# A first load split in two halves over two issuing engines, in a recurrence followed by a soft mixture of experts

## Chip, cores and metric

The kernel runs on one core of one Trainium2 chip. The metric is the device time of one execution in microseconds (us). A core has a matrix engine (PE, TensorE), a vector engine (DVE, VectorE), a scalar engine (ACT, ScalarE), a general engine (POOL, GpSimd) and a synchronising engine (SP, SyncE) that does no arithmetic. Transfers between the chip's memory and the on-chip buffer of 128 partitions are issued by SP, ACT or POOL, each with a queue of its own, and carried out by 16 DMA engines.

## The reference

Two layers in a row. The first is a gated recurrence over 5056 tokens for each of 4 sequences and 256 channels, the second a soft mixture of 8 experts with 4 slots each over all 20224 tokens.

```
x: (4, 5056, 256)   f_logit: (4, 5056, 256)   lower_bound: (256)
phi: (256, 32)      w1: (8, 256, 1024)        w2: (8, 1024, 256)      all float32

sig = 1 / (1 + exp(-f_logit))
f   = lower_bound + (1 - lower_bound) * sig
i   = 1 - f
h   = 0
for t in range(5056):
    h = f[:, t] * h + i[:, t] * x[:, t]
    y[:, t] = h

x = y.reshape(20224, 256)
logits = x @ phi
d = softmax of logits over the tokens
slot_input = d.T @ x
for each expert e:  slot_out[e] = relu(slot_input[e] @ w1[e]) @ w2[e]
c = softmax of logits over the 32 slots
out = c @ slot_out
```

## The kernel before

**Tiling.** The tokens of each sequence are cut into groups of 512 (128 partitions times 4 tokens). One group of one sequence is a unit; units are numbered with the sequence running fastest, 40 in all. A pair of units shares a tile of `f_logit` (`f_t`) and a tile of `x` (`x_t`), each 128 partitions by 2 by 4 by 256 values in float32; three tiles of each kind are in rotation. The first six units (`SINGLE`, L318) are loaded one at a time: one transfer of 512 KB for each half of a tile, 128 rows of 4 KB. In the middle a transfer brings a whole pair, 1 MB, and a group near the end has a shape of its own.

**What a unit passes through.** `gate` (L227): ACT takes the sigmoid of `-f_logit` into `s_t`. `enter` (L237): `u_t = s_t * x_t`, on DVE in two parts for unit 0, on POOL for the others. `s_to_channels` and `u_to_channels`: PE transposes both so that channels lie on partitions. `decay` (L286): ACT turns the transposed sigmoid into the decay `a` with a scale taken from `lower_bound` and a bias of 1. `scan` (L306): DVE runs the recurrence. `to_tokens`, `keep_tokens`, `logits`, `exps`, `weights_to_tokens` and `slots` then build the softmax over the tokens and gather the slot inputs on PE, ACT and DVE.

**Constants.** `lower_bound` comes as a row of 256 values, `lb_row`, by a transfer that ACT issues at L75, at the start of the program. `lb_constants` (L104) transposes that row with two small PE instructions (L109) and makes `omlb` and `nomlb`, the two signs of `1 - lower_bound`, with two DVE instructions (L110, L111). `decay` scales with `nomlb`; `phi_constants` (L113) multiplies `phi`, which POOL loads at L79, by `omlb`.

**Loads.** `load(n, k)` (L204) runs over `f_logit` and `x` in that order and issues every load from SP. For the first units it is the last branch, L224 and L225. A load into a tile in rotation is issued when the tile's last reader is done with it. Weights are loaded by POOL (`load_w`, L135), cast to bf16 on the way, at units listed in `W_AT`; the last two second-layer weights use a tile of `f_t`'s rotation and are named `w_t`.

**Order.** The order on each engine is written out by hand; each engine runs its instructions in program order and waits for semaphores. At the beginning (L462 on) all six single loads are issued on SP, twelve transfers in the order f, x, f, x; then follow `lb_constants`, `gate(0)`, `enter(0)`, `s_to_channels(0)`, the first half of `decay(0)`, `u_to_channels(0)`, `gate(1)`, and so on. On ACT's queue the issue of `lb_row` is therefore followed by the loading of the function table for the sigmoid and then by the sigmoid of unit 0. On PE the two transposes of `lb_row` come ahead of those of `s_t`; on DVE the two constants come ahead of unit 0's multiply.

**The end.** When the last weights are there, PE finishes `so_ps` (L669), DVE and POOL make `slot_out` and `slot_bd` (L683, L685), and the output is formed block by block: a matmul, a scaling on DVE or ACT, and a store issued by SP (L724, L744, L763, L789, L806).

Of the kernel before, what the change touches and what calls it, by code (L numbers as in the profile page):

```python
# [18 lines left out]
def kernel(  # L19
# [10 lines left out]
    nc = tc.nc  # L30
# [5 lines left out]
    P = 128  # L36
# [9 lines left out]
    def first(g):  # L46
        return g * G if g < n_grp - 1 else S - G
# [24 lines left out]
    rep = consts.tile([P, B, NS], F32, name="rep")  # L72

    lb_row = consts.tile([1, D], F32, name="lb_row")
    nc.scalar.dma_start(out=lb_row, in_=lower_bound.unsqueeze(0))  # L75
    lbs = consts.tile([P, 2, DC], F32, name="lbs")
    omlb, nomlb = lbs[:, 0], lbs[:, 1]
    phi_f = consts.tile([P, DC, NS], F32, name="phi_f")
# [25 lines left out]
    def lb_constants():  # L104
        row = lb_row.rearrange("u (p o) -> u p o", o=DC)
        lb_ps = ptp.tile([P, R, P], F32, name="lb_ps", tag="tp")
        lb = lb_ps[:, 0, ds(0, DC)]
        for o in range(DC):
            nc.tensor.transpose(lb_ps[:, 0, ds(o, 1)], row[:, :, o], ident_f[ds(0, 1), ds(0, 1)])  # L109
        nc.vector.tensor_scalar(omlb, lb, -1.0, 1.0, ALU.mult, ALU.add)  # L110
        nc.vector.tensor_scalar(nomlb, lb, 1.0, -1.0, ALU.mult, ALU.add)  # L111
# [50 lines left out]
    with tc.tile_pool(name="sp2", bufs=3) as sp2, \  # L162
# [24 lines left out]
        def long(n):  # L187
            return 2 * B <= n < n_unit - 2 * B

        def place(n):  # L190
            if long(n):
                t, j = divmod(n, 2 * B)
                return 2 * t + j % 2, j // 2
            return divmod(n, B)
# [4 lines left out]
        def tokens(src, n, k):  # L199
            g, b = divmod(n, B)  # L200
            v = src[ds(b, k), ds(first(g), G)]
            return v.rearrange("b (p r) d -> p b r d", r=R)

        def load(n, k=2):  # L204
            for src, dst, tag in ((f_logit, fs, "f_t"), (x, xs, "x_t")):
                if n % 2 == 0:
                    dst[n // 2] = ld.tile([P, 2, R, D], F32, name=tag, tag=tag)
                t = dst[n // 2]
                if long(n):
                    g, b = place(n)  # L210
                    nc.sync.dma_start(
                        out=t.rearrange("p u r d -> p (u r) d"),
                        in_=src[b, ds(first(g), 2 * G)].rearrange("(p r) d -> p r d", r=2 * R))
                elif n // B == odd:
                    b, t0 = n % B, first(odd)
                    nc.sync.dma_start(
                        out=t[:, 0, R3],
                        in_=src[ds(b, 2), ds(t0 + P * R3, L)].rearrange("b t d -> t b d"))
                    for m in range(2):
                        nc.sync.dma_start(  # L220
                            out=t[:, m, ds(0, R3)],
                            in_=src[b + m, ds(t0, P * R3)].rearrange("(p r) d -> p r d", r=R3))
                else:
                    for m in range(n, n + k):  # L224
                        nc.sync.dma_start(out=t[:, ds(m % 2, 1)], in_=tokens(src, m, 1))  # L225

        def gate(n, k=2):  # L227
            if n % 2 == 0:
                sts[n // 2] = sp2.tile([P, 2, R, D], BF16, name="s_t", tag="s_t")
            s_t, f_t = sts[n // 2][:, ds(n % 2, k)], fs[n // 2][:, ds(n % 2, k)]  # L230
            if n // B == odd:
                m = (R + R3) * D
                s_t = s_t.rearrange("p u r d -> p (u r d)")[:, :m]
                f_t = f_t.rearrange("p u r d -> p (u r d)")[:, :m]
            nc.scalar.activation(s_t, f_t, ACT.Sigmoid, scale=-1.0)  # L235
# [225 lines left out]
        SETTLED = 3 * B  # L461
        for n in range(SINGLE):  # L462
            load(n, 1)
        lb_constants()
        gate(0, 1)
        enter(0)
# [12 lines left out]
        for n in range(n_unit):  # L479
            if n < SINGLE - 2:  # L480
# [9 lines left out]
                if n % 2 == 0:  # L490
                    unit(load, n + AHEAD)
                unit(enter, n + 3)
                rep_constants(n)
            else:
                end = n >= n_unit - 6
                if n % 2 == 0:
                    unit(load, n + AHEAD)
                    if n == SINGLE - 2:
                        to_tokens(n - 1)
                        keep_tokens(n - 1)  # L500
                    if not end and n >= SETTLED:
                        unit(gate, n + 4)
                else:
                    unit(decay, n + 1)
                    if n < SETTLED:
                        gate(n + 3)
                    if n == n_unit - 5:
                        gate(n + 3)
                        exps(odd - 1)
# [85 lines left out]
    with tc.tile_pool(name="ew", bufs=1) as ew, \  # L595
# [34 lines left out]
        for q in range(E // Q):  # L630
# [4 lines left out]
            if q == 0:  # L635
                nc.tensor.matmul(cs_ps, rep2, cs1, start=True, stop=True)
                src = ht_ps.rearrange("p f (j s) -> p f j s", s=NS)[:, :, :, ds(0, SPE)]
                src = bass.AP(tensor=src.tensor, offset=src.offset,
                              ap=[list(src.ap[0]), [P, FC], [NS + SPE, Q], [1, SPE]])
# [6 lines left out]
            for j in range(Q):  # L646
                s0 = (Q + j) * SPE
                src = ht_ps[:, :, ds(j * NS + s0, SPE)]
# [18 lines left out]
        for j in range(Q):  # L667
# [8 lines left out]
            if j == 1:  # L676
                row_sums(2)
                spin(unread, 4, D)
                q = n_grp * R - 1
# [164 lines left out]
```

## Time and profile before

| | us |
|---|---|
| median of 3 runs | 198.03 (197.97 to 198.04) |
| the profiled execution | 198.15 |
| its span, first to last instruction | 196.4 |
| PE busy | 151.1 (77%) |
| DVE busy | 142.3 (72%) |
| ACT busy | 138.4 (70%) |
| POOL busy | 103.2 (53%) |
| mean granted TensorE clock | 0.851 |
| memory read | 58.23 MB |
| memory written | 20.71 MB |
| f_t transfers of 512 KB, median from issue to landing | 8.3 |
| x_t transfers of 512 KB, median from issue to landing | 9.9 |

The span runs from the first to the last instruction of the profiled execution; its time is 1.75 us longer than that, and this rest lies outside the trace. Busy shares are averages over the whole span. DMA time is not that of an engine: a transfer is issued by an instruction of 0.3 to 0.5 us on a queue (SPq, ACTq) and lands later; the share of the DMA engines says how busy the 16 of them were on average. It can read slightly above 1.

Lines in the views name the operation as out<-in with a line number of the program, so `s_t<-f_t` at L235 is the sigmoid. In the square brackets of a timeline stands how long the engine was idle before, and what ended it.

### The profile page before, as it was taken

The page shows a single profiled execution, that of the slowest core. Times are in us where ns is not written, and L with a number is a line of the kernel's source. Part 1 is how long each engine was busy: PE and PEld are TensorE (multiplying, and loading weights), DVE is VectorE, ACT ScalarE, POOL GpSimd, SP SyncE. Part 2 cuts the span into 40 slices and gives each one's busy share as a digit, 9 for nine tenths or more (in the row PEclk, how much of TensorE's full clock was granted, in tenths as well). Part 3 has the DMA queues.
Part 4 walks back from the last instruction along what each step waited for, and adds up shares of the span by engine and source line. Part 5 has one row for each costly group of instructions (what it writes and reads, how often), then busy time and mean ns, then how long its engine had stood idle before and what let it go on. Part 6 is the DMA issues. An engine that isn't in the chain of part 4 may idle for free.

```text
span 196.4 us, 3226 instructions
## 1 busy us (share of the span) xinstructions
PE 151.1 (77%) x1195; PEld 106.5 (54%) x1195; DVE 142.3 (72%) x167; ACT 138.4 (70%) x193; POOL 103.2 (53%) x78
## 2 busy tenths in 40 slices
PE   0687599887999979898897978999796999950000
PEld 0475468675777757666695857568562533310000
DVE  2669769999799999999989999432187868740000
ACT  3688677899899999999897798331077699980000
POOL 2689577874998588884969978192030000000000
PEclk9999769996999999999999999999995555555555
DMA  5999999999999999999999999999749999999995
GB/s 204 419 416 423 422 429 421 429 429 358 380 426 426 397 345 426 424 413 314 401 419 406 249 217 214 213 214 214 142 149 426 425 450 424 427 427 427 427 427 217
DMA packets 14161, 70.75 MB, mean 360 GB/s; under 512 B 1585, under 2 KB 2866, under 8 KB 10178
## 3 DMA queue, kind: packets, MB, share of 16 engines
q1 hardware_dynamic: 11520, 62.13, 76.3%
q0 software_dynamic: 2624, 8.42, 21.5%
q8 instruction: 9, 0.15, 0.3%
q14 instruction: 6, 0.05, 0.1%
q10 hardware_dynamic: 2, 0.00, 0.0%
HBM read 58.23 MB, written 20.71 MB: 402 GB/s over the span
## 4 chain that ended last, share of the span: by engine, by line
PE 34%; DMA 23%; DVE 18%; POOL 7%; issue 4%; ACT 2%; ACTq 0%; DVEq 0%; POOLq 0%
DVE h L313 11%; PE op L775 10%; DMA w_sb<-in_moe_w_dram 7%; DMA w_t<-in_moe_w_dram 7%; DMA x_t<-in_x_dram 7%; POOL u_t L246 6%; PE hp L326 5%; PE sp L261 5%; PE up L267 4%; DVE ht L345 3%; DVE oc L692 2%; PE slot_ps L183 2%; PE lg L359 2%; DMA f_t<-in_f_logit_dram 2%; PE op L702 2%
## 5 line engine op out<-in xcount | busy, mean ns | idle before, releaser
L246 POOL TENSOR_TENSOR u_t<-s_t,x_t 128x1024 bf16<-128x1024 bf16 (+1 forms) x39 | 82.5, 2130 | 22.6 <-ACT s_t L235 12.7
L313 DVE TENSOR_TENSOR_SCAN h<-a,h,up 128x512 bf16<-128x512 f32 (+1 forms) x72 | 86.8, 1252 | 4.5 <-PE up L267 2.2
L235 ACT ACTIVATE s_t<-f_t 128x2048 bf16<-128x2048 f32 (+2 forms) x23 | 38.3, 1668 | 4.9 <-DMA f_t<-in_f_logit_dram 4.7
L326 PE MATMUL hp<-ident_f,h 128*128 128x128 f32 (+1 forms) x160 | 29.4, 308 | 7.9 <-DVE ht L345 6.6
L326 PEld LDWEIGHTS hp<-ident_f,h 128*128 128x128 f32 (+1 forms) x160 | 23.5, 207 | 19.0 <-DVE ht L345 12.6
L261 PE MATMUL sp<-ident_f,s_t 128*128 128x128 f32 x144 | 22.1, 298 | 6.8 <-ACT s_t L235 4.5
L295 ACT ACTIVATE a<-sp,lbs 128x1024 f32<-128x1024 bf16 x24 | 25.4, 1114 | 0.9 <-PE sp L261 0.6
L261 PEld LDWEIGHTS sp<-ident_f,s_t 128*128 128x128 f32 x144 | 18.1, 155 | 8.6 <-ACT s_t L235 5.0
L302 ACT ACTIVATE a<-sp,lbs 128x512 f32<-128x512 bf16 (+2 forms) x22 | 17.8, 858 | 4.7 <-PE sp L261 4.4
L775 PE MATMUL op<-slot_bd,etall 64*128 64x512 bf16 x48 | 19.3, 621 | 0.0
L267 PE MATMUL up<-ident_f,u_t 64*128 64x64 f32 x192 | 17.8, 231 | 1.8 <-POOL u_t L246 1.8
L786 ACT ACTIVATE oc<-op,rrow 128x256 f32<-128x256 f32 x48 | 18.2, 492 | 1.1 <-PE op L775 0.5
L780 DVE TENSOR_TENSOR oc<-op,rrow 128x1024 f32<-128x1024 f32 x12 | 14.5, 1223 | 4.3 <-PE op L775 4.3
L183 PE MATMUL slot_ps<-rep,ident_f 128*128 128x256 f32 x52 | 17.5, 432 | 0.0
L267 PEld LDWEIGHTS up<-ident_f,u_t 64*128 64x128 f32 x192 | 14.1, 139 | 5.7 <-POOL u_t L246 2.1
L345 ACT COPY ht<-hp 128x512 f32<-128x512 f32 (+1 forms) x20 | 11.6, 582 | 5.2 <-PE hp L326 5.1
L345 DVE COPY ht<-hp 128x512 f32<-128x512 f32 (+1 forms) x20 | 13.4, 668 | 1.3 <-PE hp L326 1.3
L696 ACT ACTIVATE ob<-op,rrow 128x256 f32<-128x256 f32 x15 | 5.8, 478 | 11.4 <-PE op L702 11.3
L775 PEld LDWEIGHTS <-etall 64*128 64x128 bf16 x48 | 7.2, 158 | 11.6 <-issue 10.3
L313 DVE TENSOR_TENSOR_SCAN h<-a,up 128x512 bf16<-128x512 f32 x8 | 9.3, 1208 | 2.4 <-PE up L261 2.4
L359 PE MATMUL lg<-h,phi 128*32 128x512 bf16 (+1 forms) x80 | 9.8, 412 | 0.3 <-ACT et L383 0.2
L261 PE MATMUL up<-ident_f,u_t 128*128 128x128 f32 x48 | 9.4, 328 | 0.5 <-POOL u_t L246 0.5
(114 smaller groups left out, 162.7 us busy)
## 6 DMA issues: line engine op xcount, KB each, us to landing
f_t<-in_f_logit_dram SPq DMA_DIRECT2D x12, 1024.0 KB, 12.3
x_t<-in_x_dram SPq DMA_DIRECT2D x12, 1024.0 KB, 11.2
out_dram<-oc SPq DMA_DIRECT2D x6, 2048.0 KB, 11.5
w_sb<-in_moe_w_dram POOLq DMA_DIRECT2D x14, 512.0 KB, 10.5
f_t<-in_f_logit_dram SPq DMA_DIRECT2D x12, 512.0 KB, 8.3
x_t<-in_x_dram SPq DMA_DIRECT2D x12, 512.0 KB, 9.9
out_dram<-oc SPq DMA_DIRECT2D x4, 896.0 KB, 6.5
out_dram<-ob SPq DMA_DIRECT2D x1, 2048.0 KB, 8.7
```

What stands on the lines that cost most here:

```text
L183: nc.tensor.matmul(slot_bank[:, 1], ident_f, wide_rep, start=False, stop=False, skip_group_check=True)
L235: nc.scalar.activation(s_t, f_t, ACT.Sigmoid, scale=-1.0)
L246: nc.gpsimd.tensor_tensor(uts[n][:, :r], s_t[:, :r], x_t[:, :r], ALU.mult)
L261: nc.tensor.transpose(ps[:, :, r], t[:, r], ident_f)
L267: nc.tensor.transpose(v[:, :, r], t(r)[k].bitcast(F32), ident_f[k, k])
L295: nc.scalar.activation(a, sp[:, :, :, :, o], ACT.Identity, scale=nomlb[:, ds(o, 1)], bias=1.0)
L302: nc.scalar.activation(decays[n // 2, o][:, ds(n % 2, k), :T], sp[:, ds(n % 2, k), :T, o], ACT.Identity, scale=nomlb[:, ds(o, 1)], bias=1.0)
L313: nc.vector.tensor_tensor_scan(h[:, :T, o], decays[n // 2, o][:, n % 2, :T], up[:, :T, o], hs[number(g - 1, b)][:, ds(used(g - 1) - 1, 1), ...
L326: nc.tensor.transpose(hp[:n_p, r], hw[:, :n_p, r], ident_f)
L345: copy(hts[g][:n_p, b].rearrange("p r d -> p (r d)").bitcast(F32), hps.pop(n)[:n_p].rearrange("p r c -> p (r c)"))
L775: nc.tensor.matmul(op[:, i_r].rearrange("p u d -> p (u d)"), ew[:, :, r + i_r], slot_bd[ds(j * 2 * NS, 2 * NS)].rearrange("s u d -> s (u d)"),
L786: nc.scalar.activation(ob[:, u, r + i_r], op[:, i_r, u], ACT.Copy, scale=scale[:, r + i_r, ds(u, 1)])
```

## The change

The first load, that of unit 0's `f_logit` tile, goes as two transfers of 64 rows. SP issues the one for partitions 0 to 63 and ACT the one for partitions 64 to 127. The issue of `lower_bound`, so far ACT's first, stands behind the loads of the first six units in the program, so on ACT it comes behind the second half. The rows of 4 KB, the bytes moved, the eleven other first loads and all computation stay as they are. `gate(0)`, which reads the tile, now depends on two transfers.

```diff
     lb_row = consts.tile([1, D], F32, name="lb_row")
-    nc.scalar.dma_start(out=lb_row, in_=lower_bound.unsqueeze(0))
     lbs = consts.tile([P, 2, DC], F32, name="lbs")
...
+                elif n == 0 and src is f_logit:
+                    for q, half in ((nc.sync, ds(0, P // 2)), (nc.scalar, ds(P // 2, P // 2))):
+                        q.dma_start(out=t[half, ds(0, 1)], in_=tokens(src, 0, 1)[half])
                 else:
                     for m in range(n, n + k):
                         nc.sync.dma_start(out=t[:, ds(m % 2, 1)], in_=tokens(src, m, 1))
...
         for n in range(SINGLE):
             load(n, 1)
+        nc.scalar.dma_start(out=lb_row, in_=lower_bound.unsqueeze(0))
         lb_constants()
```

## The prediction

> **What bounds the kernel now.** I read the busy times by stage first, because the page's averages (PE 77%, DVE 72%, ACT 70%) name no engine. Columns: stretch and length in us, busy time of PE, its weight loads, DVE, ACT and POOL with instruction counts, granted TensorE clock, mean busy share of the 16 DMA engines, GB/s.
>
> ```profile
> 0.00:2.40 2.40, 0.00 (x0) 0.00 (x0) 0.92 (x16) 1.14 (x1) 1.42 (x7) 1.00 0.18 14
> 2.40:5.00 2.60, 0.39 (x2) 0.31 (x2) 0.45 (x3) 0.81 (x2) 0.00 (x0) 1.00 0.94 377
> 5.00:40.00 35.00, 28.32 (x171) 21.60 (x171) 28.85 (x29) 26.91 (x30) 26.13 (x17) 0.90 1.02 425
> 40.00:80.00 40.00, 36.75 (x343) 28.57 (x341) 37.52 (x36) 38.09 (x37) 32.19 (x17) 0.96 1.02 398
> 80.00:113.00 33.00, 29.60 (x262) 22.96 (x261) 32.40 (x32) 29.26 (x30) 27.10 (x19) 1.00 1.03 373
> 113.00:140.80 27.80, 24.86 (x313) 18.72 (x313) 15.90 (x24) 13.22 (x22) 14.49 (x18) 1.00 1.06 211
> 140.80:144.80 4.00, 3.50 (x32) 2.89 (x31) 1.80 (x4) 1.22 (x4) 1.62 (x2) 1.00 0.13 23
> 144.80:194.00 49.20, 27.67 (x83) 11.48 (x80) 24.43 (x27) 27.76 (x74) 0.21 (x1) 0.53 1.00 421
> ```
>
> From about 2.5 to 140.8 the DMA share is 0.94 to 1.06 in every stage. (The 211 GB/s of the weight stage counts only the bf16 that is written; twice that, 422, is read.) At 144.8 the stores take over, full again to the end. So the time is one full stream of loads, a gap of 4.0 us in which the last weights become the slot outputs, and one full stream of stores. What makes the load stream start later or run slower moves the end by as much; what only makes an engine later doesn't, while transfers are queued.
>
> Next the chain of waits (start, length, what), for what the early compute is worth:
>
> ```profile
> 0.72 3.60 DMA f_t<-in_f_logit_dram
> 4.34 1.07 ACT s_t L235
> 5.45 1.13 PE sp L261 x4
> ...
> 20.53 13.69 DMA x_t<-in_x_dram
> ...
> 113.08 14.35 DMA w_sb<-in_moe_w_dram
> 127.72 14.34 DMA w_t<-in_moe_w_dram
> ```
>
> The chain begins with the very load that is changed. But the x load issued at 20.53 lands 13.69 us later, and moving its 1 MB takes 2.5 us at the stage's 425 GB/s: some 11 us are waiting in the queue. If the early compute is 1 us late, that load is issued 1 us later and waits 1 us less. The other end closes likewise: the last two weight pieces land at 14 us, and PE finds its work waiting for them.
>
> Last, the first microseconds, in order of time:
>
> ```profile
> 0.72 0.51 ACTq L75 DMA_DIRECT2D lb_row<-in_lower_bound_dram  x1
> 0.72 0.38 SPq L225 DMA_DIRECT2D f_t<-in_f_logit_dram  x1
> 1.16 0.42 SPq L225 DMA_DIRECT2D x_t<-in_x_dram  x1
> 1.26 1.28 ACT L235 ACT_TABLE_LOAD   x1 [1.26 <-PEq L828]
> 4.34 1.06 ACT L235 ACTIVATE s_t<-f_t 128x1024 bf16<-128x1024 f32 x1 [1.79 <-DMA f_t<-in_f_logit_dram]
> 5.69 1.29 DVE L242 TENSOR_TENSOR u_t<-s_t,x_t 128x512 bf16<-128x512 bf16 x2 [2.59 <-DMA x_t<-in_x_dram]
> ```
>
> and cut finer, for the first packets:
>
> ```profile
> 1.60:1.62 0.02, 0.00 (x0) 0.00 (x0) 0.02 (x1) 0.02 (x1) 0.02 (x1) 1.00 0.14 51
> 2.40:2.46 0.06, 0.02 (x1) 0.02 (x1) 0.04 (x1) 0.06 (x1) 0.00 (x0) 1.00 0.00 0
> 2.46:2.48 0.02, 0.02 (x1) 0.02 (x1) 0.02 (x1) 0.02 (x1) 0.00 (x0) 1.00 1.57 614
> ```
>
> 51 GB/s for 0.02 us is 1 KB: I read that as lower_bound's packet, 0.88 after its issue. The packets of f start at 2.46, 1.74 after theirs. From there the first tile is 512 KB, 1.25 us at 419 GB/s, to 3.7, and counts as landed at 4.32; the later early tiles let their readers go 1.25 to 1.35 us apart (ACT starts on f at 9.41 and 11.92, with one x between).
>
> **The change part by part.** The sum is made against the profiled execution: 198.15 us, a span of 196.4 and 1.75 around it; the median of the runs is 0.12 below it, 198.03.
>
> *Issue on SP.* The half replaces the whole at the head of SP's queue. The trace has issues of 512 KB at 0.38, of 1 MB at 0.33 and of a single row at 0.51 (on ACT): the duration doesn't follow the size. So x still goes at about 1.16, and all eleven loads behind it as before: 0.
>
> *Issue on ACT.* The second half takes the place of lower_bound at 0.72, at that row's 0.51, and lower_bound follows from 1.23 to 1.74. Behind them on ACT stands the table load, now 1.74 to 3.02 instead of 1.26 to 2.54. Its cover is the wait for f: ACT idles 1.79 ahead of 4.34, so 1.3 remain: 0. Without that cover the price is the 0.51.
>
> *lower_bound's landing.* Soonest 0.88 after its issue, at 2.1; latest behind the half on ACT's queue, one packet after f itself. It feeds two transposes (PE, 0.39) and two DVE instructions (0.16 and 0.15). On PE they stand ahead of the transposes of s, which wait until 5.45, 1.1 after f is there; on DVE ahead of the multiply at 5.69. Even the latest landing fits into these waits, 0.7 against 1.1: 0. Uncovered, it would be some 0.7 on the early compute, which the 11 us of queue swallow.
>
> *A second semaphore for the first sigmoid.* Semaphore instructions in the trace take 0.02 to 0.05; they lie on the early compute: 0 at the end.
>
> *The stream itself.* The same 512 KB in the same 4 KB rows, but as two transfers that reach 64 partitions each. No row of before shows such a transfer; all its large ones reach 128. From below: if the late start of f, 0.86 beyond that of the one-row transfer, belongs to the size of the transfer, half the rows save half of it: -0.43. A counter-row: the first stores, 128 rows of 1 KB, go at 144.04 and their first traffic is in the stretch from 144.84, 0.80 later, so the number of rows is not it; 4 KB rows or a cold read would be, and halves keep both. From above: if a half uses only half of the paths that a whole one uses, each half takes the 1.25 of the whole, together 2.5 instead of 1.25: +1.25. If the two interleave evenly, 0. Between, I take +0.62: half of the worst price, because x is queued behind SP's half from 1.16 and can fill part of what the halves leave idle; and no gain at the start, by the counter-row.
>
> [...]
>
> Sum: 198.15 + 0.62 = 198.77, less 0.12 for the median: **198.65**.
>
> **The rivals.**
>
> *Slower in full.* Both halves go packet by packet in step, never on both sets of paths at once, and nothing of x fills in: +1.25, 199.28. For it: nothing in the queue passes a transfer ahead of it on the same queue. Against it: two queues that start at different moments need not stay in step. [...]
>
> *No change.* The packets merely take another queue, at the rate of before: 198.03, within 0.3. For it: the stage holds share 1.02 with transfers of 512 KB, 1 MB and weights from another queue mixed. Against it: all of those reach 128 partitions. That the halves do nothing because one is issued late belongs here too: x is behind SP's half, so the stream stays fed, f lands later and only the early compute moves. It turns into a loss only when lateness passes the 11 us of queue.
>
> *Not slower but faster: the stream starts sooner.* Place: before 2.46, where the DMA engines stand idle. If ACT's half starts its packets 0.88 after its issue, as lower_bound's did, at 1.6 rather than 2.46, the first 256 KB (0.62 us at full rate) are through before SP's half begins; bounded by that 0.62, and by the saving of 0.43 worked out above. I take 0.43: 197.60. It decides if the first packet comes before about 2.05 with the rate at once as high as now. PE waits 0.55, 0.21 and 0.26 for the last three weight pieces, so the compute behind the stream can follow about this much. For it: the 0.88. Against it: the counter-row, and a half at half rate eats the gain.
>
> [...]
>
> **How the numbers follow.** A run of this kernel tells about 0.2%, 0.4 us, from no change. Chances: the forecast at half price 0.36, slower in full 0.12, no change 0.27, a sooner start 0.25. Slower is therefore 0.48, same 0.27, faster 0.25. The likeliest one's own range is 198.45 to 199.1. With the other cases it reaches from 197.5 (a little beyond the sooner start) to 199.3 (the full price).
>
> **What would show it.** Right: the stretch from 2.4 to 5.0 moves clearly less than 377 GB/s, the first sigmoid starts near 5.0 and the first multiply near 6.3, the last weights land 0.6 later than 142.06, and gap and stores keep their 4.0 and 49.2. No change: first packets at 2.46, 377 GB/s, sigmoid within 0.3 of 4.34. Sooner start: packets on ACT's queue near 1.6 at over 300 GB/s, and the last weights 0.4 earlier. The steps costed at nothing are wrong if PE or DVE waits for lower_bound after s or x is there, or if the sigmoid waits for the table load. The whole reading is wrong if the load stream starts and runs as before and the end still moves: then it would lie in the gap, the stores or the clock.

## The result: 0.84 us slower

The changed kernel takes 198.81 us (median of 9 runs) against 197.97 us for the kernel before (9 runs beside them). The ratio over all runs is 1.0059, with a 95% interval of 1.0040 to 1.0077; that of the two medians alone is 1.0042. Medians in this document count every run, while the ratios leave out the runs that lie far off: four of e1 (202.5 to 205.3 us), one each of e4 (422.91) and e9 (201.75), and one of the kernel before beside e1 to e4 (266.32). The profiled execution of the changed kernel took 199.35 us with a span of 197.5, so it lies 0.54 above its own median; that of before lay 0.12 above, and the two profiled executions differ by 1.20. Its runs also spread more: 198.6 to 199.55 and one of 200.52, where all but one of before's lie within 0.16.

The busy times by stage of the changed kernel, with the columns of the prediction's first view (length, PE, its weight loads, DVE, ACT, POOL, clock, DMA share, GB/s):

```profile
0.00:2.40 2.40, 0.00 (x0) 0.00 (x0) 0.92 (x16) 0.00 (x0) 1.42 (x7) 1.00 0.27 41
2.40:5.00 2.60, 0.00 (x0) 0.00 (x0) 0.23 (x1) 0.00 (x0) 0.00 (x0) 1.00 0.95 237
5.00:40.00 35.00, 24.82 (x168) 19.53 (x168) 28.43 (x30) 28.02 (x31) 25.10 (x17) 1.00 1.02 421
113.00:140.80 27.80, 24.59 (x308) 18.32 (x307) 16.56 (x24) 13.88 (x23) 15.16 (x19) 1.00 1.06 214
140.80:144.80 4.00, 3.34 (x29) 2.48 (x29) 0.56 (x2) 0.00 (x0) 0.39 (x1) 1.00 0.34 57
144.80:194.00 49.20, 29.05 (x94) 12.72 (x92) 25.67 (x29) 28.99 (x76) 1.45 (x2) 0.54 0.98 413
```

The DMA engines are as busy as before from 2.4 to 5.0 (0.95, was 0.94), yet move 237 GB/s instead of 377. Later the old rate is back: 421 GB/s from 5 to 40 (was 425; the last slow packets are still in it), 398 and 378 from 40 to 80 and to 113 (398 and 373), 214 in the weight stage (211). In 140.8 to 144.8 there are still loads (57 GB/s, was 23): the stream ends later.

The same view cut finer, first the kernel before:

```profile
2.40:3.40 1.00, 0.39 (x2) 0.31 (x2) 0.45 (x3) 0.15 (x1) 0.00 (x0) 1.00 0.82 332
3.40:5.20 1.80, 0.00 (x0) 0.00 (x0) 0.00 (x0) 0.86 (x1) 0.00 (x0) 1.00 1.02 404
5.20:7.00 1.80, 1.55 (x6) 1.00 (x6) 1.29 (x2) 0.59 (x2) 1.03 (x1) 1.00 1.05 429
7.00:10.00 3.00, 1.84 (x7) 1.01 (x6) 2.17 (x2) 2.40 (x4) 2.15 (x3) 1.00 1.03 422
```

and the changed one:

```profile
2.40:3.40 1.00, 0.00 (x0) 0.00 (x0) 0.23 (x1) 0.00 (x0) 0.00 (x0) 1.00 0.67 242
3.40:5.20 1.80, 0.00 (x0) 0.00 (x0) 0.00 (x0) 0.00 (x0) 0.00 (x0) 1.00 1.03 217
5.20:7.00 1.80, 0.37 (x2) 0.31 (x2) 0.23 (x2) 1.41 (x2) 0.70 (x2) 1.00 1.02 401
7.00:10.00 3.00, 2.01 (x8) 1.42 (x8) 1.29 (x2) 1.79 (x3) 0.00 (x0) 1.00 1.03 421
```

Two readings come out of such a row and are used for every experiment below.

- **Engine time of a packet**: the 16 engines times their share, divided by the rate, per 4 KB. Before, 3.4 to 5.2: 16 x 1.02 x 4.096 / 404 = 0.165 us. Changed: 16 x 1.03 x 4.096 / 217 = 0.311 us. The packets take almost twice as long.
- **Loss of the stream**: the bytes missing from the rows, at 420 GB/s. 90 KB in the first row, 337 in the second, 50 in the third, 3 in the last, less the 65 KB that the changed kernel moved more before 2.4: 415 KB, 0.99 us. How exact this is can be read from the kernels below whose start isn't slow (e2, e4, e7 and e9 to e11): the same sum up to 10 us gives -12 to 52 KB, at most 0.12 us.

That loss is still there at the end of the loads. From the chain of waits of the changed kernel (start, length, what):

```profile
0.72 4.79 DMA f_t<-in_f_logit_dram
22.14 13.28 DMA x_t<-in_x_dram
113.74 14.71 DMA w_sb<-in_moe_w_dram
128.74 14.56 DMA w_t<-in_moe_w_dram
```

The last weight lands at 143.30 instead of 142.06, 1.24 later. From there to the last instruction it is 54.2 us, and was 54.3: neither the gap nor the stores lose anything. Nor does the clock: its mean is 0.868, and was 0.851. The start in order of time:

```profile
0.72 0.60 SPq L224 DMA_DIRECT2D f_t<-in_f_logit_dram  x1
0.73 0.56 ACTq L224 DMA_DIRECT2D f_t<-in_f_logit_dram  x1
1.32 0.77 ACTq L466 DMA_DIRECT2D lb_row<-in_lower_bound_dram  x1
1.38 0.80 SPq L227 DMA_DIRECT2D x_t<-in_x_dram  x1
2.22 0.43 SPq L227 DMA_DIRECT2D f_t<-in_f_logit_dram  x1
5.53 0.37 PE L108 MATMUL lb_ps<-ident_f,lb_row 1*128 1x1 f32 x2 [5.53 <-DMA lb_row<-in_lower_bound_dram]
5.58 1.28 ACT L237 ACT_TABLE_LOAD   x1 [5.58 <-DMA f_t<-in_f_logit_dram]
6.88 1.06 ACT L237 ACTIVATE s_t<-f_t 128x1024 bf16<-128x1024 f32 x1
7.97 1.29 DVE L244 TENSOR_TENSOR u_t<-s_t,x_t 128x512 bf16<-128x512 bf16 x2 [1.81 <-ACT s_t L237]
```

The issue of a half takes 0.56 to 0.60, longer than that of the whole (0.38), and the two behind it are stretched too (0.77 and 0.80, against 0.51 for `lb_row` and 0.42 for x before). The function table is now loaded behind the wait for f, from 5.58 to 6.86, not in its shadow (1.26 to 2.54 before). The first sigmoid starts 2.54 later than before. Which of these the end pays for is the question of the experiments.

### The profile page after: what moved, and what is told of

Its sections match the earlier page's. It is cut to its first block, busy times and chain, and to the rows that moved or that the text cites. A ratio compares the mean times of both kernels' runs of the same rounds, so it can differ in the third digit from the quotient of the medians.

```text
span 197.5 us, 3228 instructions
## 1 busy us (share of the span) xinstructions
PE 148.0 (75%) x1195; PEld 104.5 (53%) x1195; DVE 142.2 (72%) x167; ACT 138.0 (70%) x193; POOL 102.2 (52%) x78
## 4 chain that ended last, share of the span: by engine, by line
PE 32%; DMA 24%; DVE 18%; POOL 6%; ACT 5%; issue 3%; ACTq 0%; DVEq 0%; POOLq 0%
DVE h L315 11%; PE op L778 10%; DMA w_sb<-in_moe_w_dram 7%; DMA w_t<-in_moe_w_dram 7%; DMA x_t<-in_x_dram 7%; POOL u_t L248 5%; PE sp L263 5%; PE hp L328 5%; PE up L269 4%; DVE ht L347 3%; DVE oc L695 2%; DMA f_t<-in_f_logit_dram 2%; ACT a L304 2%; ACT s_t L237 2%; PE slot_ps L182 2%
## 5 line engine op out<-in xcount | busy, mean ns | idle before, releaser
L263 PE MATMUL sp<-ident_f,s_t 128*128 128x128 f32 x144 | 20.9, 288 | 5.0 <-ACT s_t L237 3.3
L263 PEld LDWEIGHTS sp<-ident_f,s_t 128*128 128x128 f32 x144 | 17.3, 149 | 6.4 <-ACT s_t L237 3.8
L182 PE MATMUL slot_ps<-rep,ident_f 128*128 128x256 f32 x52 | 17.0, 422 | 1.0 <-POOL rep L85 1.0
L182 PEld LDWEIGHTS slot_ps<-rep,ident_f 128*128 128x128 f32 x52 | 8.3, 193 | 3.0 <-POOL rep L85 1.2
```

Source lines behind the costliest of these rows:

```text
L182: nc.tensor.matmul(slot_bank[:, 1], ident_f, wide_rep, start=False, stop=False, skip_group_check=True)
L263: nc.tensor.transpose(ps[:, :, r], t[:, r], ident_f)
```

## Experiments

Twelve runs were made, two of them repetitions, each timed against the kernel before in the same session; the ratio is that to before. Diffs are against the changed kernel unless said otherwise.

### Whose loss: the late compute or the stream

**e7: the unchanged loads, the compute late** (diff against the kernel before).

```diff
-            nc.scalar.activation(s_t, f_t, ACT.Sigmoid, scale=-1.0)
+            for _ in range(3 if n == 0 else 1):
+                nc.scalar.activation(s_t, f_t, ACT.Sigmoid, scale=-1.0)
```

> The kernel before, with the first sigmoid done three times into the same tile, so that all compute of unit 0 starts some 2.1 us later; no transfer is changed. Theory that the load stream sets the end and the queue swallows a late start: 198.0, within 0.2. Rival, that the changed kernel lost by its late compute (its first sigmoid started at 6.88 instead of 4.34): 198.5 to 200.1.

197.96 us against 198.00; ratio 0.9998 (0.9989 to 1.0006). Unit 0's compute starts late:

```profile
4.32 3.23 ACT L236 ACTIVATE s_t<-f_t 128x1024 bf16<-128x1024 f32 x3 [1.77 <-DMA f_t<-in_f_logit_dram]
7.60 1.12 PE L262 MATMUL sp<-ident_f,s_t 128*128 128x128 f32 x4 [4.76 <-ACT s_t L236]
```

The first transposes start at 7.60 instead of 5.45, close to the changed kernel's 7.99, and the end doesn't move. So neither the later landing of f nor the displaced table load is what the changed kernel pays for.

**e8 and e12: the table load brought forward.** A sigmoid of one column, on a small new tile, right behind the issue of `lower_bound`. The same kernel was run twice.

```diff
+    warm = consts.tile([P, 2], F32, name="warm")
+    nc.vector.memset(warm, 0.0)
...
         nc.scalar.dma_start(out=lb_row, in_=lower_bound.unsqueeze(0))
+        nc.scalar.activation(warm[:, ds(0, 1)], warm[:, ds(1, 1)], ACT.Sigmoid, scale=-1.0)
```

> The changed kernel with a sigmoid of one column on ACT right behind the issue of lower_bound, so that the table load comes at 2 instead of waiting for f until 5.58. The first sigmoid then starts about 1.3 us earlier. Theory of the load stream: no gain, 198.6 to 198.8, and 2.4 to 5.0 still near 240 GB/s. Rival (late compute): 0.5 to 1.2 us less than the changed kernel.

> The changed kernel with the early table load once more, since its first time, 200.55, lost steadily through the whole load stream (2.3 us by the weights, 0.8 of it in the first 2 MB), with all packets 1 to 2% longer. If that belongs to where the buffers lay at that time, it comes now near the changed kernel, 198.6 to 199.4; if to the early table, 200.4 again.

200.55 us, ratio 1.0131 (1.0118 to 1.0144), and the second time 200.58, 1.0125 (1.0104 to 1.0147). Both theories missed: it is some 1.8 us slower than the changed kernel although its first sigmoid started at 5.41 in e8. The edit changes something else. In e12 the stream is slower long after the start:

```profile
12.00:15.00 3.00, 2.94 (x13) 2.54 (x14) 1.79 (x2) 2.66 (x5) 2.30 (x2) 1.00 1.01 406
15.00:18.00 3.00, 3.00 (x16) 2.87 (x15) 3.00 (x4) 2.64 (x5) 2.77 (x3) 1.00 1.02 406
```

The same rows of before have 421 at a share of 1.03 and 416 at 1.02, so a packet takes 0.163 to 0.165 instead of 0.160 to 0.161. My guess that it hung on where the memory lay in one session isn't borne out by the second run. The new tile is 8 bytes in each partition and is made ahead of the tiles that the loads write; whether it moved them, and whether their place matters, wasn't tried, nor the tile without the early sigmoid. As a test of the late compute these two runs are confounded; e7 stands for it.

### What makes the packets slow: two queues, few rows, or which rows

**e1: the changed kernel once more.**

> The changed kernel once more, for a second profile and for the spread of its runs (198.6 to 199.6 and one 200.5 so far, against 197.9 to 198.1 before). Either theory expects 198.6 to 199.5. If the spread comes from how the two halves meet at the start, this profile's stretch 2.4 to 5.0 differs from the first one's 237 GB/s together with the end; if it comes from later, the stretch is the same and only the end differs.

198.68 us against 198.10; ratio 1.0023 (1.0007 to 1.0038): slower again, by less than the first time. The two intervals don't overlap, so the size of the loss is known only as something between 0.14 and 1.5 us. The profile that this run left, of an execution of 203.20 us, isn't used, and the question about the spread stays open.

**e2: halves by columns**, 128 rows of 2 KB each, still from SP and ACT.

```diff
-                    for q, half in ((nc.sync, ds(0, P // 2)), (nc.scalar, ds(P // 2, P // 2))):
-                        q.dma_start(out=t[half, ds(0, 1)], in_=tokens(src, 0, 1)[half])
+                    for q, half in ((nc.sync, ds(0, R // 2)), (nc.scalar, ds(R // 2, R // 2))):
+                        q.dma_start(out=t[:, 0, half], in_=tokens(src, 0, 1)[:, 0, half])
```

> Halves by columns instead of rows: each transfer has 128 rows of 2 KB, still one from SP and one from ACT. Theory of the paths (64 partitions reach only half of them): the slow stretch goes away, packets at full rate from about 2.7, 198.0 to 198.2. Theory of the two queues (two transfers issued at the same moment hinder each other, whatever rows they have): as slow as the changed kernel, 198.6 to 199.5.

198.00 us, ratio 0.9993 (0.9982 to 1.0005): nothing lost.

```profile
3.40:5.20 1.80, 0.37 (x2) 0.31 (x2) 0.04 (x1) 0.81 (x1) 0.00 (x0) 1.00 1.05 421
```

Full rate, and both issues took 0.38 and 0.41. Two transfers from two queues at the same moment are not the trouble. Nor do they gain anything.

**e4: the whole load from ACT**, SP starting with x at the same moment.

```diff
-                    for q, half in ((nc.sync, ds(0, P // 2)), (nc.scalar, ds(P // 2, P // 2))):
-                        q.dma_start(out=t[half, ds(0, 1)], in_=tokens(src, 0, 1)[half])
+                    nc.scalar.dma_start(out=t[:, ds(0, 1)], in_=tokens(src, 0, 1))
```

> The whole first load from ACT, 128 rows, SP starting with x at the same moment. Theory of the paths: no half, so full rate, 197.9 to 198.2 (f and x share the engines, both land near 5.5). Theory of the two queues: SP and ACT still issue at the same moment, so a slow stretch and 198.5 to 199.5.

198.22 us against 198.10, ratio 1.0000 (0.9984 to 1.0015). f and x, both issued at 0.72, are on their way together, the first sigmoid waits until 6.11 (4.34 before), and the end stays.

**e3: both row halves from SP**, `lower_bound` first on ACT as before.

```diff
-                    for q, half in ((nc.sync, ds(0, P // 2)), (nc.scalar, ds(P // 2, P // 2))):
+                    for q, half in ((nc.sync, ds(0, P // 2)), (nc.sync, ds(P // 2, P // 2))):
```

> Both row halves from SP, one behind the other, lower_bound first on ACT as before. Theory of the paths: each half at half rate, the stretch 2.4 to 5.0 well under 377 GB/s and 198.6 to 199.2. Theory of the two queues: only one more issue of 0.4 us, 198.0 to 198.2.

199.68 us against 198.10, ratio 1.0077 (1.0046 to 1.0108).

```profile
3.40:5.20 1.80, 0.00 (x0) 0.00 (x0) 0.00 (x0) 0.00 (x0) 0.20 (x1) 1.00 1.05 222
```

One queue, and the same slow packets (0.310 us). By the same sum the stream loses 1.40 us (60 + 328 + 178 + 3 KB, and 19 before 2.4), more than in the changed kernel, and the time is 0.5 above the range that I expected; why one queue pays more isn't shown. The row halves carry the price, not the queues and not the place of `lower_bound`.

**e5: even and odd partitions** instead of lower and upper ones, from SP and ACT.

```diff
-                    for q, half in ((nc.sync, ds(0, P // 2)), (nc.scalar, ds(P // 2, P // 2))):
+                    for q, half in ((nc.sync, slice(0, P, 2)), (nc.scalar, slice(1, P, 2))):
```

> The halves take the even and the odd partitions instead of the lower and the upper 64: as many rows, bytes and transfers as in the changed kernel, one from SP and one from ACT, but each half reaches all over the partitions. Theory of the paths: full rate in 2.4 to 5.0 (340 to 380 GB/s) and 197.9 to 198.2. Rival, that 64 rows make a transfer slow whichever they are (the issue of one took 0.56 to 0.60 us against 0.38): 210 to 260 GB/s and 198.6 to 199.5.

199.21 us against 198.00, ratio 1.0066 (1.0052 to 1.0079): slow, against my theory. But by another way:

```profile
3.40:5.20 1.80, 0.37 (x2) 0.31 (x2) 0.23 (x2) 0.67 (x1) 0.27 (x1) 1.00 0.85 326
5.20:7.00 1.80, 0.07 (x1) 0.07 (x2) 0.00 (x0) 1.67 (x2) 0.43 (x2) 1.00 0.85 310
```

The packets are nearly as fast as before (16 x 0.85 x 4.096 / 326 = 0.171 us), but the engines are idle for 15% of the time. SP's own queue, from its fourth issue on:

```profile
2.69 0.69 SPq L227 DMA_DIRECT2D x_t<-in_x_dram  x1
3.43 0.46 SPq L227 DMA_DIRECT2D f_t<-in_f_logit_dram  x1
3.93 0.97 SPq L227 DMA_DIRECT2D x_t<-in_x_dram  x1
4.95 1.07 SPq L227 DMA_DIRECT2D f_t<-in_f_logit_dram  x1
6.06 0.55 SPq L227 DMA_DIRECT2D x_t<-in_x_dram  x1
```

By 6.0 SP has issued seven transfers; before it had issued ten. But work wasn't short: the six loads whose issue was over by 4.9 are 3.1 MB, and 1.0 MB had moved by 5.2. So why the engines idle isn't shown. Slow packets or idle engines: the next three runs look at the two cuts away from the start of the stream.

### The price by itself, in the full stream

In these the first load is whole, as before, and the ninth (unit 4's f, moving near 12 us, with the queue full) is cut, all pieces from SP. Diff against the kernel before; e10 has `(slice(0, P, 2), slice(1, P, 2))` and e11 `(ds(i * P // 4, P // 4) for i in range(4))` in its place.

```diff
+                elif n == 4 and src is f_logit:
+                    for part in (ds(0, P // 2), ds(P // 2, P // 2)):
+                        nc.sync.dma_start(out=t[part, ds(0, 1)], in_=tokens(src, 4, 1)[part])
```

> The kernel before with its first load whole again, but unit 4's f load, the ninth, in two row halves (partitions 0 to 63, then 64 to 127), both from SP. It moves near 12 us, far into the saturated stream. Theory of a price per row half (packets at half rate): slow packets near 12 us, the stream 0.7 to 1.4 us late from there, 198.7 to 199.6. Rival, that the loss belongs to the start of the stream: 198.0, within 0.2.

> The same ninth load as even and odd partitions, both from SP. The lower and upper halves had slow packets, even and odd partitions had none but left gaps in the stream. If slow packets (two engines on one path) are the price and the gaps came from the start, 198.0 to 198.2. If any transfer of 64 rows costs the stream time, 198.6 to 199.4.

> The same ninth load as four transfers of 32 rows, all from SP. If the price is half rate for these 512 KB, it is as in two halves, 198.7 to 199.6. If the price is paid per transfer, it doubles or more: 199.4 to 201. If the loss belongs to the start: 198.0 to 198.2.

The kernel before, in these stretches:

```profile
12.00:15.00 3.00, 3.00 (x17) 2.92 (x16) 3.00 (x4) 2.72 (x4) 2.66 (x2) 1.00 1.03 421
15.00:18.00 3.00, 2.21 (x17) 1.70 (x16) 3.00 (x4) 2.65 (x5) 2.79 (x3) 1.00 1.02 416
```

Lower and upper halves (e9): 199.36 us against 198.08, ratio 1.0073 (1.0047 to 1.0099).

```profile
12.00:15.00 3.00, 2.88 (x17) 2.54 (x17) 3.00 (x4) 2.21 (x3) 2.35 (x2) 1.00 1.04 306
15.00:18.00 3.00, 1.27 (x9) 0.84 (x8) 3.00 (x4) 2.06 (x3) 1.89 (x3) 1.00 1.02 391
```

Even and odd partitions (e10): 197.84 us, ratio 0.9995 (0.9979 to 1.0012).

```profile
12.00:15.00 3.00, 3.00 (x16) 2.88 (x15) 3.00 (x4) 2.29 (x4) 2.70 (x2) 1.00 1.02 407
15.00:18.00 3.00, 2.05 (x17) 1.79 (x16) 3.00 (x4) 2.82 (x4) 2.45 (x3) 1.00 1.03 422
```

Quarters (e11): 199.11 us, ratio 1.0055 (1.0036 to 1.0074).

```profile
12.00:15.00 3.00, 3.00 (x17) 2.88 (x17) 3.00 (x4) 2.21 (x3) 2.06 (x2) 1.00 1.05 294
15.00:18.00 3.00, 1.24 (x9) 0.81 (x8) 2.65 (x4) 1.70 (x3) 1.92 (x3) 1.00 0.99 344
```

e9 loses (115 + 25) x 3 = 420 KB, 1.00 us of stream, at a full share: slow packets, as in the changed kernel. e10 loses 24 KB and no time: as many rows, as many transfers, the same long issues (1.55 for the two), but partitions from all over. So what costs is that a transfer covers 64 neighbouring partitions, and with a full queue the long issue is free. Neighbouring partitions are also neighbouring rows of 4 KB in memory; on which of the two sides the price arises, no run separates. e11 loses 597 KB, 1.42 us of stream, of which the end shows some 1.0. The price is not per transfer, since doubling their number doesn't double it.

Which packets are slow shows when e9's trace is divided by bytes. Each of these rows moves 254 to 263 KB, about the size of a half, and the first begins where the eight loads ahead have been moved; taking the packets in the order of the queue (before, the first four loads landed in that order, at 4.3, 5.6, 7.0 and 8.2), they are the two halves and then the next load:

```profile
12.65:13.37 0.72, 0.72 (x6) 0.72 (x5) 0.72 (x2) 0.72 (x2) 0.45 (x1) 1.00 1.11 353
13.37:14.47 1.10, 0.97 (x7) 0.74 (x7) 1.10 (x2) 0.93 (x2) 0.72 (x1) 1.00 1.03 238
14.47:15.52 1.05, 1.05 (x8) 0.85 (x8) 1.05 (x2) 0.00 (x0) 1.05 (x1) 1.00 0.98 246
15.52:16.15 0.63, 0.28 (x3) 0.20 (x3) 0.63 (x2) 0.21 (x1) 0.60 (x2) 1.00 1.04 417
```

A packet takes 0.21 us in the first half, 0.28 in the second, 0.26 in the first half of the whole load of x behind it, and 0.16 after that. The half that goes first pays little; the second one and the neighbour behind it, which wasn't cut, pay the rest.

**e6: unit 0's x cut by rows as well**, the suspected price twice.

```diff
-                elif n == 0 and src is f_logit:
+                elif n == 0:
```

> Unit 0's x is split by rows too, in the same way: the suspected cost twice. Theory of the paths (a price per row half): the loss doubles, 1.2 to 2.0 us, 199.2 to 200.0. Rival, a price paid once at the start because two queues begin at the same moment: as the changed kernel, 198.6 to 198.8.

199.79 us against 198.00, ratio 1.0092 (1.0079 to 1.0105).

```profile
3.40:5.20 1.80, 0.00 (x0) 0.00 (x0) 0.00 (x0) 0.00 (x0) 0.00 (x0) 1.00 1.06 232
5.20:7.00 1.80, 0.00 (x0) 0.00 (x0) 0.00 (x0) 1.30 (x2) 0.00 (x0) 1.00 1.04 226
7.00:10.00 3.00, 1.78 (x8) 1.31 (x8) 1.38 (x4) 1.38 (x2) 1.12 (x1) 1.00 0.99 371
```

The slow stretch is twice as long and its loss, by the same sum (82 + 310 + 365 + 153 KB, less 31 before 2.4), is 2.09 us, against 0.99. The end moves by 1.8. The price is paid for each of the two tiles that are cut.

None of the twelve runs beats the kernel before: e2, e4, e7 and e10 are equal to it within their intervals.

## Why the prediction was right, point by point

**What bounds the kernel: right.** The load stream sets the end. e7 and e4 move the early compute by about 2 us and change nothing; e3, e6 and e9 make the stream late by 1.0 to 2.1 and the end follows by 1.2 to 1.8. It doesn't follow to the tenth: e11's stream lost 1.42 and its end 1.0. From the landing of the last weight to the last instruction it is 53.8 to 54.4 us in the profiles of e2 to e12, so most of the difference arises earlier: in e5, for instance, the stream lost 0.87 at its start and the last weight landed 1.78 later. What adds to it there was not settled.

**The term for the stream: right in place and direction; its size was partly luck.** I put 0.62, half of the full price of 1.25, hoping that x would fill in what the halves leave idle. x didn't fill in, it was slowed too: the rate stays at 217 GB/s to 5.2, when x is moving. The measured term is 0.99 of stream, four fifths of the full price. The median moved by 0.84, between my forecast and the rival "slower in full"; the repetition e1 moved by 0.58, just below the forecast. The full price itself supposed that each half alone uses half of the paths and takes 1.25. In e9 the first half took 0.72, the second 1.10, and the first half of x behind them 1.05, where 0.62 each would be full rate. So one error of the working, that x would escape, was offset by another, that the first half would pay. That a half uses half of the paths, from which the price of 1.25 and so the 0.62 are worked out, was only supposed: no run shows it, nor the two engines on one path of e10's expectation, and it explains neither the fast first half nor the slow start of the whole load behind. What the runs show in its place is the time of a packet, 0.311 us against 0.165, a loss of 0.99 us of stream in the changed kernel and 1.00 in e9, and that it matters which rows of the tile a piece covers: 306 and 391 GB/s with 64 neighbouring ones (e9), 407 and 422 with every second one (e10).

**The issue on SP, costed at 0 because its length "doesn't follow the size": wrong in the length.** A half takes 0.60, not 0.38, and x goes at 1.38, not 1.16. In a full queue that is free (e10: 1.55 for the two, ratio 0.9995). At the start of the stream it may not be: e5 has fast packets and still loses 0.87, with idle engines, though whether the issues cause that isn't shown. In the changed kernel the share is 1.03 while the packets are slow, so there the engines aren't idle.

**The table load, costed at 0 under the wait for f: the cover wasn't there, the 0 for the end was right.** It ran at 5.58, behind the wait, instead of 1.74 to 3.02. Where the first sigmoid waits for one transfer it stands ahead of the wait (before at 1.26, e4 at 1.73); where it waits for two, behind (4.39 in e2, 5.58 here). So the sigmoid came at 6.88, not near 5.0, and the multiply at 7.97, not 6.3. By the prediction's own sign, "if the sigmoid waits for the table load", this step was wrong, and the 0.51 that it named for the uncovered case was not the price either: the sigmoid started 1.30 after f was there. That the end doesn't pay for it is shown by e7, where transposes that start at 7.60 instead of 5.45 leave the end where it was.

**lower_bound: right.** It landed with f, PE took it at 5.53, and PE's next work came at 7.99.

**The rival of a sooner start: its ground was misread.** I took 2.46 for f's first packet. In the kernel before there is earlier traffic:

```profile
1.76:1.78 0.02, 0.00 (x0) 0.00 (x0) 0.02 (x1) 0.02 (x1) 0.02 (x1) 1.00 6.15 410
1.94:1.96 0.02, 0.00 (x0) 0.00 (x0) 0.01 (x1) 0.02 (x1) 0.02 (x1) 1.00 4.19 410
```

410 GB/s for 0.02 us is two packets of 4 KB, and a share of 6.15 of 16 engines is 16 x 6.15 x 0.02 / 2 = 0.98 us for each. The trace puts them on SP's queue: they are f's own first rows, 1.04 after the issue, close to the 0.88 of lower_bound. There was no late start to save. Nor are the first packets always long: in e9, whose start is that of before, the packets up to 2.40 take 0.17 us each (55 GB/s at a share of 0.14), and the long ones come between 2.40 and 3.40 (266 at 0.90, 0.22 us). What makes them long wasn't tested. e2, where the two halves go at full rate, gains nothing.

## What to carry to other kernels

Cut a transfer by columns, so that each piece still covers all 128 partitions (e2: 421 GB/s, ratio 0.9993), and not into blocks of neighbouring ones: here each tile of 512 KB cut in such blocks cost 1.0 to 1.4 us of a saturated stream. Every second partition was free inside a full queue (e10, ratio 0.9995), but not at the start (e5, 1.0066). With some 11 us of transfers queued, a first tile whose compute started 2 us late cost nothing (e7, ratio 0.9998), while a loss of 0.99 us in the stream itself came with an end 0.84 later. Read the DMA share together with the rate: the same share at half the rate means slow packets (1.03 at 217 GB/s, where it was 1.02 at 404), a lower share at nearly the same packet time means idle engines (0.85 and 0.171 us in e5, 1.02 and 0.165 before), and issues that come later don't yet explain those.

## What was not expected of the hardware

- The issue of a transfer got longer with fewer rows: the first one of the program took 0.38 to 0.41 with 128 rows (e2's halves by columns and e4 too) and 0.56 to 0.60 with 64. In a full queue two of 64 rows took 1.55 together, and four of 32 rows 4.06.
- The half that is served first runs fast. In the changed kernel the packets between 2.4 and 3.4 take 16 x 0.67 x 4.096 / 242 = 0.18 us, and only then 0.31. e9 shows the same order in a full stream. Why the price falls on the second half and on the transfer behind it is open.
- A tile of 8 bytes per partition, added ahead of the load tiles, and a sigmoid of one column on it went with packets some 2% slower for the first 40 us (from 40 to 80 the rate is 395 GB/s against 398) and some 1.8 us more time than without them, in two sessions. The cause wasn't tested.
